# Token-direction sums in plain float32 on four 32-column groups, in place of split fp32r sums that pass through DRAM

## The chip, the cores and the metric

The kernel runs on one core of one Trainium2 chip. The metric is the time on the device in microseconds, from one launch; smaller is better. A measured time is the median over runs; the profile is of one execution.

## The reference

Three stages follow each other: a linear attention, a gated convolution block ("moe"), and a mixing block ("moe2"). The change lies where the second stage ends and the third begins.

```python
# stage 1: B, H, S, D = 4, 8, 576, 64; d_feat = 128
num = einsum('bhsf,bhfd->bhsd', phi(q), einsum('bhsf,bhsd->bhfd', phi(k), v))
x   = (num / den) laid out as [4, 576, 512]
# stage 2: d_ff = 1024
h = maximum(x @ w_in, 0);  c = 3-tap convolution of h along the tokens
x = (h * sigmoid(c)) @ w_out                      # [4, 576, 512]
# stage 3: rank R = 32, hidden 2048
u = x + ((x^T @ U) @ V)^T                         # U [576, 32], V [32, 576]
out = u + maximum(u @ w_ch1, 0) @ w_ch2
```

`x^T @ U` sums over all 576 tokens of a batch: for each batch it is a [32, 512] table, here called the token sums T = U^T x. It must be complete before the first row of u of that batch can be made.

## The kernel before

**Number formats.** Most matmuls run in fp32r, a one-pass format that keeps fewer bits; to keep float32 accuracy each operand is split into a high and a low part, and three products (high·high, high·low, low·high) are summed. A matmul on plain float32 operands is also used, in the attention stage; the trace shows it as two matmul instructions for each call in the program.

**Tiles.** The 4 x 576 = 2304 tokens are 18 tiles of 128 rows, 9 for a pair of batches: four tiles of the even batch, one middle tile whose first 64 rows belong to the even batch and last 64 to the odd one, and four tiles of the odd batch.

**Stage 2** is a loop over n = 0..31 (4 batches of 8 blocks of 128 hidden features). In round n `moe_in(n)` makes a block of h, and two rounds later `out_and_sums(n)` calls `moe_out(n)`, which adds the block into four PSUM tiles `x2p`. After the eighth block of a batch `x2_rows` copies each finished tile with ACT to an SBUF tile `x2` and sends it to DRAM (`x2d`). The middle tile of a pair is made by `moe_out_middle` in PSUM tile `x2m`, from the held pieces `ghold`, after the odd batch.

**The token sums before.** `split_t` takes one waiting x2 tile per round, makes its high part `x2h` on ACT and its low part `x2l` on DVE. `flush_t`, in the next round, multiplies: U's tile with its high and low halves side by side (64 columns) against `x2h`, then U's high half (32 columns) against `x2l`, into one PSUM tile `tp`, whose 64 rows DVE copies or adds into the accumulator `tacc` ([64, 512]; two of them, one for even and one for odd batches). For the middle tile this happens twice, once for each batch. When a batch is complete, `tacc` is stored to DRAM (`td`) by a DMA on SP's queue; `load_tstack` loads it back with its two halves side by side into a staging tile `ta`, adds the halves (`tf`), and writes the fp32r stack `tst` (high, low, high) that `mix` multiplies with V.

**Around the seam.** After the loop, stage 3 runs in 5 blocks of 4, 4, 4, 4 and 2 tiles. `mix(i, t)` computes the mixed rows in PSUM tile `ups` and DVE adds them to `u`; `turn(i, t)` transposes `u` on PE into `utp`, and ACT and DVE split it into `uh` and `ul`; `up` and `down` are the two large products (`hps`, and `po`). `between(i, s)` is called between them and places `mix`, `turn`, the last sums and `load_tstack(2)`, `load_tstack(3)`. `tp` shares the two PSUM buffers of `ps_u` with `ups` and `utp` here; in stage 2 it shares the one buffer of `ps_t` with `x2m`.

**Order.** PE's order is that of the program text from the attention stage through the first pass over the blocks (`tc.manual_schedule`). The orders on DVE, ACT and SP's DMA queue are chosen by the framework's planner from its own estimate of times, and each of them is then run strictly in that order. Weights for stage 3 are decoded by `ch_piece`, eight pieces early, in stage 2, and the rest later (`decode`); each piece takes one buffer of the staging tags `raw` and `x` (two buffers each), the same that `load_tstack` uses for `ta` and `tf`.

Of the kernel before, what the change touches and what calls it, by code (L numbers as in the profile page):

```python
# [8 lines left out]
F32 = mybir.dt.float32  # L9
F32R = mybir.dt.float32r  # L10
# [8 lines left out]
P = 128  # L19
# [5 lines left out]
def kernel(  # L25
# [15 lines left out]
    nc = tc.nc  # L41

    B, H, S, D = 4, 8, 576, 64
    DM = H * D
    FF = w_in.shape[1]
    HID = w_ch1.shape[1]
    R = U.shape[1]
    NK = DM // P
    NJ = FF // P
# [8 lines left out]
    cpool = ctx.enter_context(tc.tile_pool(name="cpool", bufs=1))  # L58
    dpool = ctx.enter_context(tc.tile_pool(name="dpool", bufs=1, space=DRAM))
    wpool = ctx.enter_context(tc.tile_pool(name="wpool", bufs=8, side="right"))  # L60
    stage = ctx.enter_context(tc.tile_pool(name="stage", bufs=2))
# [3 lines left out]
    make_identity(nc, ident)  # L65

    cw = cpool.tile([P, 3 * NJ], F32, name="cw")
    us = [cpool.tile([P, 5, 2 * R], F32R, name=f"us{i}") for i in range(2)]

    td = [dpool.tile([2 * R, DM], F32, name=f"td{b}") for b in range(B)]  # L70
    x2d = [dpool.tile([P, DM], F32, name=f"x2d{i}") for i in range(NT)]
    NU = B * H // 4
    PT = 2 * S
# [71 lines left out]
    def load_us(odd):  # L145
        if odd:
            parts = [
                (everything, slice(R, 5 * R), U[LEFT:S].rearrange("(t p) r -> p t r", p=P)),
                (slice(LEFT, P), slice(0, R), U[0:LEFT]),
            ]  # L150
            zero = (slice(0, R),)
        else:
            parts = [
                (everything, slice(0, 4 * R), U[0:MAIN].rearrange("(t p) r -> p t r", p=P)),
                (slice(0, LEFT), slice(4 * R, 5 * R), U[MAIN:S]),
            ]
            zero = (slice(4 * R, 5 * R),)
        f = load_small(P, 5 * R, f"us{odd}", parts, zero).rearrange("p (t r) -> p t r", r=R)
        nc.vector.tensor_copy(us[odd][:, :, 0:R], f)
        nc.vector.tensor_sub(us[odd][:, :, R : 2 * R], f, us[odd].bitcast(F32)[:, :, 0:R])  # L160

    def split_steps(src, hi, lo, name, engine):

# [101 lines left out]
    raw, state, xt = {}, {}, {}  # L265
# [298 lines left out]
    i = NU - 1  # L564
# [20 lines left out]

    vpool = ctx.enter_context(tc.tile_pool(name="vpool", bufs=1, side="right"))
    vst = vpool.tile([3 * R, S + P], F32R, name="vst")
    taccs = [vpool.tile([2 * R, DM], F32, name=f"tacc{i}") for i in range(2)]
    moe_ctx = ExitStack()
    mpool = moe_ctx.enter_context(tc.tile_pool(name="mpool", bufs=1, side="right"))  # L590
    ps_x = moe_ctx.enter_context(tc.tile_pool(name="ps_x", bufs=4, space=PSUM))
    ps_t = moe_ctx.enter_context(tc.tile_pool(name="ps_t", bufs=1, space=PSUM))
# [43 lines left out]
    def x2_rows(b, gt, ps):  # L636
        if b == B - 1 and gt % 9 > 4:
            x2 = x2_last[:, gt % 9 - 5, :]
        else:
            x2 = mpool.tile([P, DM], F32, tag="x2", name=f"x2_{gt}", bufs=5)  # L640
        nc.scalar.copy(x2, ps)
        nc.sync.dma_start(out=x2d[gt], in_=x2)
        t_todo.append((b, gt, x2))

    def moe_out(n):
        b, j = divmod(n, NJ)
        if j == 0:
            x2p[:] = [ps_x.tile([P, 512], F32, tag="x", name=f"x2p{b}_{t}") for t in range(4)]
        g = gs.pop(n)
        off = LEFT * (b % 2)  # L650
        rest = MAIN - off * (MAIN // LEFT)
        nc.gpsimd.tensor_copy(  # L652
            ghold[:, :, j, off : off + LEFT], g.bitcast(F32)[:, :, rest : rest + LEFT]
        )
        w = [wout[j // 2][:, x, (j % 2) * 512 : (j % 2) * 512 + 512] for x in range(2)]
        for t in range(4):
            ts_ = slice(off + t * P, off + (t + 1) * P)
            for i, (gi, wi) in enumerate(((0, 0), (0, 1), (1, 0))):
                nc.tensor.matmul(  # L659
                    x2p[t], lhsT=g[:, gi, ts_], rhs=w[wi],  # L660
                    start=(j == 0 and i == 0), stop=(j == NJ - 1 and i == 2),
                )
        if j == NJ - 1:
            for t in range(4):
                x2_rows(b, (b // 2) * 9 + (b % 2) * 5 + t, x2p[t])

    middle = {}

    def moe_out_middle(pair, js):
        if pair not in middle:  # L670
            middle[pair] = ps_t.tile([P, 512], F32, tag="t", name=f"x2m{pair}")
        ps = middle[pair]
        for j in js:
            for gi, wi in ((0, 0), (0, 1), (1, 0)):
                nc.tensor.matmul(  # L675
                    ps, lhsT=ghold[:, gi, j, :], rhs=wout[j // 2][:, wi, (j % 2) * 512 : (j % 2) * 512 + 512],
                    start=(j == 0 and gi + wi == 0), stop=(j == NJ - 1 and gi == 1),
                )
        if js[-1] == NJ - 1:
            x2_rows(2 * pair + 1, 9 * pair + 4, ps)  # L680

    t_todo = []

    t_split = []

    def split_t(pool, bufs):
        if t_todo:

            t_todo.sort(key=lambda e: e[1])
            b, gt, x2 = t_todo.pop(0)  # L690
            xh = pool.tile([P, DM], F32R, tag="x2h", name=f"x2h_{gt}", bufs=bufs)
            xl = pool.tile([P, DM], F32R, tag="x2l", name=f"x2l_{gt}", bufs=bufs)
            nc.scalar.copy(xh, x2)
            nc.vector.tensor_sub(xl, x2, xh.bitcast(F32))
            t_split.append((b, gt, xh, xl))

    def flush_t(psum, tag):
        if t_split:
            b, gt, xh, xl = t_split.pop(0)
            r = gt % 9  # L700
            if r < 4:
                parts = [(b, us[0][:, r, :], r == 0)]
            elif r == 4:
                parts = [(b - 1, us[0][:, 4, :], False), (b, us[1][:, 0, :], True)]
            else:
                parts = [(b, us[1][:, r - 4, :], False)]
            for bb, ut, first in parts:
                tacc = taccs[bb % 2]
                pt = psum.tile([P, 512], F32, tag=tag, name=f"tp{gt}_{bb}")
                nc.tensor.matmul(pt[0 : 2 * R], lhsT=ut, rhs=xh, start=True, stop=True)  # L710
                nc.tensor.matmul(pt[0:R], lhsT=ut[:, 0:R], rhs=xl, start=False, stop=True, skip_group_check=True)
                if first:
                    nc.vector.tensor_copy(tacc, pt[0 : 2 * R])
                else:
                    nc.vector.tensor_add(tacc, tacc, pt[0 : 2 * R])
                if (r == 4 and bb == b - 1) or r == 8:
                    nc.sync.dma_start(out=td[bb], in_=tacc)

    def load_vst():
        for c in range(2):  # L720
# [8 lines left out]
    tstack = []  # L729

    def load_tstack(b):
        ta = stage.tile([P, 2, DM], F32, tag="raw", name=f"ta{b}")[0:R]
        nc.sync.dma_start(out=ta, in_=td[b].rearrange("(a r) d -> r a d", a=2))
        tf = stage.tile([P, DM], F32, tag="x", name=f"tf{b}")[0:R]
        nc.vector.tensor_add(tf, ta[:, 0, :], ta[:, 1, :])
        st = vpool.tile([3 * R, DM], F32R, tag="tst", name=f"tst{b}", bufs=2)
        nc.vector.tensor_copy(st[0:R], tf)
        nc.vector.tensor_copy(st[2 * R : 3 * R], tf)
        nc.vector.tensor_sub(st[R : 2 * R], tf, st.bitcast(F32)[0:R])
        tstack.append(st)  # L740

    LAG = 2

    def out_and_sums(n):
        moe_out(n)
        if n == 2 * NJ - 1:
            moe_out_middle(0, range(NJ))
        if n < B * NJ - 1:
            flush_t(ps_t, "t")
            split_t(mpool, 2)  # L750

    early = {n: divmod(i, 2) for i, n in enumerate((9, 12, 14, 17, 20, 22, 24, 27))}
    for n in range(B * NJ):
        b, j = divmod(n, NJ)
# [29 lines left out]
    left = ctx.enter_context(tc.tile_pool(name="left", bufs=1))  # L784
    ps_u = ctx.enter_context(tc.tile_pool(name="ps_u", bufs=2, space=PSUM, side="right"))
# [45 lines left out]
    def prep(i, s):  # L831

        if 0 < s <= sizes[i]:
            turn(i, s - 1)
        if s < sizes[i]:
            mix(i, s)
# [4 lines left out]
    last, pair = B * NJ - 1, B // 2 - 1  # L841
# [64 lines left out]
    pend = None  # L906
    todo = [(j, c) for j in coming[0] for c in range(2)]

    splits, flushes = ((0, 0), (0, 5), (0, 7), (1, 5), (1, 6)), ((0, 1), (0, 6), (1, 0), (1, 6), (1, 7))

    def between(i, s):
        if (i, s) in flushes:
            flush_t(ps_u, "u")
        if (i, s) in splits:
            split_t(left, 1)
        if i + 1 < NB:
            prep(i + 1, s - 1) if s else None
        if (i, s) in ((0, 3), (1, 7)):
            load_tstack(2 + i)

    with tc.manual_schedule(engines={mybir.EngineType.PE}):
        begin(2, wpool)
# [75 lines left out]
```

## Time and profile before

| what | us |
|---|---|
| median of 3 runs | 813.12 (812.91 to 817.39) |
| span of the profiled execution | 813.1 |
| PE busy with matmuls | 797.3 (98%) |
| DVE busy | 534.4 (66%) |
| ACT busy | 360.9 (44%) |
| mean granted TensorE clock | 0.995 |

The span reaches from the first to the last instruction; the profiled execution stands within 0.1 us of the median. A PE matmul's length in the rows is its latency; matmuls overlap, so the distance between two starts is what one costs. An idle time in brackets at a row's end is what the engine waited before it, and for whom.

### The profile page before, as it was taken

The numbers are of one execution on the slowest core, as the hardware profiler recorded it, in microseconds if no ns is written. First come the engines' busy times: TensorE is split into PE (matmuls) and PEld (weight loads), VectorE is DVE, ScalarE is ACT, GpSimd is POOL, SyncE is SP. The second block draws the span as 40 slices with busy tenths as digits, with TensorE's granted clock in tenths as the row PEclk, the third lists the DMA queues.
The fourth block names the chain that finished last, engine by engine and source line by source line (L and its number), as shares of the span: only waits on it lengthen the run. The fifth ranks groups of instructions, "written<-read, shape, count | busy, mean of one in ns | idle before, by whom it ended". The sixth has DMA issues, their size and how long they took to land.

```text
span 813.1 us, 12709 instructions
## 1 busy us (share of the span) xinstructions
PE 797.3 (98%) x5086; PEld 644.6 (79%) x5086; DVE 534.4 (66%) x849; ACT 360.9 (44%) x643; POOL 120.4 (15%) x112
## 2 busy tenths in 40 slices
PE   8999999999999999999899999999999999999997
PEld 5666666669998888988678778888888888888886
DVE  5777877856999986884445795884387276231322
ACT  4778877766687564553322332441142132101010
POOL 0344445530216521110000000000000000000000
PEclk8999999999999999999999999999999999999999
DMA  7355555412212110202700231230021020000212
GB/s 228 108 166 162 160 155 170 132 32 82 67 66 92 30 69 14 69 23 71 233 8 1 65 96 34 79 104 0 29 76 52 1 78 27 0 1 1 87 69 78
DMA packets 36442, 61.27 MB, mean 75 GB/s; under 512 B 7264, under 2 KB 21728, under 8 KB 36384
## 3 DMA queue, kind: packets, MB, share of 16 engines
q1 hardware_dynamic: 36096, 60.37, 23.6%
q8 instruction: 40, 0.66, 0.3%
q14 instruction: 18, 0.15, 0.1%
q10 hardware_dynamic: 288, 0.09, 0.0%
HBM read 50.34 MB, written 10.04 MB: 74 GB/s over the span
## 4 chain that ended last, share of the span: by engine, by line
PE 58%; DVE 9%; DMA 4%; ACT 1%; issue 1%; DVEq 0%; ACTq 0%; SPq 0%
PE po L888 22%; PE hps L866 22%; PE x2p L659 6%; PE hp L611 6%; DVE cv L623 1%; PE x2m L675 1%; DMA c_5r<-in_moe_w_ch_dram 1%; DVE g L631 1%; PE utp L825 1%; DMA td<-tacc 1%; DVE u L893 1%; DMA c_0r<-in_moe_w_ch_dram 1%; DVE cv L628 1%; DMA c_4r<-in_moe_w_ch_dram 0%; DMA c_3r<-in_moe_w_ch_dram 0%
## 5 line engine op out<-in xcount | busy, mean ns | idle before, releaser
L872 ACT ACTIVATE hh<-hps 128x512 fp32r<-128x512 f32 (+1 forms) x80 | 44.2, 552 | 211.8 <-PE hps L866 207.0
L873 DVE SCALAR_TENSOR_TENSOR hl<-hps,hh 128x512 fp32r<-128x512 f32 (+1 forms) x80 | 50.6, 632 | 95.7 <-ACT hh L872 95.7
L611 PE MATMUL hp<-xh,win 128*128 128x288 f32 x512 | 105.6, 295 | 0.0
L659 PE MATMUL x2p<-wout,g 128*128 128x512 f32 x384 | 96.2, 392 | 1.6 <-ACT g L630 1.6
L866 PE MATMUL hps<-uh,c1h 128*128 128x512 f32 (+1 forms) x240 | 88.9, 370 | 1.1 <-ACT uh L828 1.1
L866 PE MATMUL hps<-ul,c1h 128*128 128x512 f32 (+1 forms) x240 | 88.5, 369 | 0.1
L866 PE MATMUL hps<-uh,c1l 128*128 128x512 f32 (+1 forms) x240 | 88.4, 368 | 0.0
L611 PEld LDWEIGHTS hp<-xh,win 128*128 128x128 f32 x512 | 84.2, 188 | 3.8 <-issue 0.5
L888 PE MATMUL po<-c2h,hh 128*128 128x512 f32 x216 | 84.3, 390 | 0.0
L888 PE MATMUL po<-c2l,hh 128*128 128x512 f32 x216 | 84.3, 390 | 0.0
L893 DVE TENSOR_TENSOR u<-u,po 128x512 f32<-128x512 f32 x90 | 58.5, 679 | 38.2 <-PE po L888 38.2
L888 PE MATMUL po<-c2h,hl 128*128 128x512 f32 x216 | 82.0, 389 | 0.0
L659 PEld LDWEIGHTS x2p<-wout,g 128*128 128x128 f32 x384 | 69.7, 188 | 14.4 <-ACT g L630 1.8
L611 PE MATMUL hp<-xl,win 128*128 128x288 f32 x256 | 75.6, 295 | 0.0
L652 POOL CAST ghold<-g 128x128 fp32r<-128x128 f32 x32 | 43.1, 1355 | 147.0 <-DVE g L631 140.9
L623 DVE SCALAR_TENSOR_TENSOR cv<-h,cw,cv 128x576 f32<-128x576 f32 x64 | 51.5, 810 | 8.9 <-ACT cv L621 8.5
L866 PEld LDWEIGHTS hps<-uh,c1h 128*128 128x128 f32 x240 | 45.2, 188 | 9.0 <-ACT uh L828 1.3
L866 PEld LDWEIGHTS hps<-ul,c1h 128*128 128x128 f32 x240 | 45.2, 188 | 8.3 <-DVE ul L829 0.5
L866 PEld LDWEIGHTS hps<-uh,c1l 128*128 128x128 f32 x240 | 45.3, 189 | 7.9
L611 PEld LDWEIGHTS hp<-xl,win 128*128 128x128 f32 x256 | 48.2, 188 | 1.2
L888 PEld LDWEIGHTS po<-c2h,hl 128*128 128x128 f32 x216 | 40.6, 188 | 8.6
L888 PEld LDWEIGHTS po<-c2l,hh 128*128 128x128 f32 x216 | 40.6, 188 | 8.0
(490 smaller groups left out, 1486.9 us busy)
## 6 DMA issues: line engine op xcount, KB each, us to landing
v<-in_v_dram SPq DMA_DIRECT2D x8, 640.0 KB, 5.7
kr<-in_k_dram SPq DMA_DIRECT2D x24, 192.0 KB, 3.7
qr<-in_q_dram SPq DMA_DIRECT2D x24, 192.0 KB, 3.8
rb<-recd SPq DMA_DIRECT2D x32, 144.0 KB, 3.7
u<-x2d SPq DMA_DIRECT2D x18, 256.0 KB, 4.2
out_dram<-u SPq DMA_DIRECT2D x18, 256.0 KB, 2.1
x2d<-x SPq DMA_DIRECT2D x14, 256.0 KB, 2.0
c_0r<-in_moe_w_ch_dram SPq DMA_DIRECT2D x2, 512.0 KB, 4.0
```

Of the source, the lines that this page charges most:

```text
L611: nc.tensor.matmul(ps[:, 0:HC], lhsT=win[kk][:, wi, j * P : (j + 1) * P], rhs=xs[b][kk][xi][:, cs], start=(i == 0), stop=(i == 3 * NK - 1),)
L623: nc.vector.scalar_tensor_tensor(out=cv, in0=h[:, t : t + S], scalar=cw[:, t * NJ + j : t * NJ + j + 1], in1=cv, op0=ALU.mult, op1=ALU.add,)
L628: nc.vector.tensor_mul(cv, cv, h[:, 1 : S + 1])
L631: nc.vector.tensor_sub(g[:, 1, :], cv, g.bitcast(F32)[:, 0, :])
L652: nc.gpsimd.tensor_copy(ghold[:, :, j, off : off + LEFT], g.bitcast(F32)[:, :, rest : rest + LEFT])
L659: nc.tensor.matmul(x2p[t], lhsT=g[:, gi, ts_], rhs=w[wi], start=(j == 0 and i == 0), stop=(j == NJ - 1 and i == 2),)
L675: nc.tensor.matmul(ps, lhsT=ghold[:, gi, j, :], rhs=wout[j // 2][:, wi, (j % 2) * 512 : (j % 2) * 512 + 512], start=(j == 0 and gi + wi == ...
L866: nc.tensor.matmul(ps[:, 0:w], lhsT=ch[j, 0][wi][:, kc], rhs=x[:, kk, :], start=(n == 0), stop=(n == 3 * NK - 1))
L872: nc.scalar.activation(hh, ps[:, 0:w], AF.Relu)
L873: nc.vector.scalar_tensor_tensor(out=hl, in0=ps[:, 0:w], scalar=0.0, in1=hh.bitcast(F32), op0=ALU.max, op1=ALU.subtract)
L888: nc.tensor.matmul(po[i][t], lhsT=x[:, cs], rhs=w, start=(j == js[0] and n == 0), stop=(j == js[-1] and n == 2))
L893: nc.vector.tensor_add(u, u, p)
```

## The change

It replaces `split_t` and `flush_t` by one helper, `token_sums`. U is kept as one plain float32 tile `us` with ten 32-column pieces. When the four tiles of a batch are done, four plain float32 matmuls are issued, each with its own 32 columns of U as weights and its own `x2` tile as moving data, and each into its own 32 partitions of one PSUM tile. DVE then copies the first 32 rows to `tacc` and adds the other three. The middle tile is one matmul with 64 columns (both batches' pieces), and two adds. `tacc` is [32, 512], and `load_tstack` reads it directly: no `td`, no `ta`, no `tf`. The calls come one round after their tiles are queued; for the last batch and the last middle tile they stand at `between(0, 1)` and `between(0, 3)`, and `load_tstack(2)` and `load_tstack(3)` both at `between(0, 3)`.

```diff
-    us = [cpool.tile([P, 5, 2 * R], F32R, name=f"us{i}") for i in range(2)]
-    td = [dpool.tile([2 * R, DM], F32, name=f"td{b}") for b in range(B)]
+    us = cpool.tile([P, 10, R], F32, name="us")
...
-        nc.vector.tensor_copy(us[odd][:, :, 0:R], f)
-        nc.vector.tensor_sub(us[odd][:, :, R : 2 * R], f, us[odd].bitcast(F32)[:, :, 0:R])
+        nc.vector.tensor_copy(us[:, 5 * odd : 5 * odd + 5, :], f)
...
-    taccs = [vpool.tile([2 * R, DM], F32, name=f"tacc{i}") for i in range(2)]
+    taccs = [vpool.tile([R, DM], F32, name=f"tacc{i}") for i in range(2)]
...
+            sums_todo.append((b, 0, t_todo[-4:]))          # in moe_out, at j == NJ - 1
...
+            sums_todo.append((2 * pair, 1, t_todo[-1:]))   # in moe_out_middle, at its end
...
-    def split_t(pool, bufs):
...
-    def flush_t(psum, tag):
...
+    def token_sums(psum, tag):
+        if not sums_todo:
+            return
+        b, both, x2s = sums_todo.pop(0)
+        pt = psum.tile([P, 512], F32, tag=tag, name=f"tp{b}_{both}")
+        if both:
+            nc.tensor.matmul(
+                pt[0 : 2 * R], lhsT=us[:, 4:6, :].rearrange("p t r -> p (t r)"), rhs=x2s[0], start=True, stop=True
+            )
+            for i in range(2):
+                nc.vector.tensor_add(taccs[i], taccs[i], pt[i * R : (i + 1) * R])
+        else:
+            for t, x2 in enumerate(x2s):
+                nc.tensor.matmul(
+                    pt[t * R : (t + 1) * R], lhsT=us[:, 6 * (b % 2) + t, :], rhs=x2, start=True, stop=True
+                )
+            tacc = taccs[b % 2]
+            nc.vector.tensor_copy(tacc, pt[0:R])
+            for t in range(1, 4):
+                nc.vector.tensor_add(tacc, tacc, pt[t * R : (t + 1) * R])
...
     def load_tstack(b):
-        ta = stage.tile([P, 2, DM], F32, tag="raw", name=f"ta{b}")[0:R]
-        nc.sync.dma_start(out=ta, in_=td[b].rearrange("(a r) d -> r a d", a=2))
-        tf = stage.tile([P, DM], F32, tag="x", name=f"tf{b}")[0:R]
-        nc.vector.tensor_add(tf, ta[:, 0, :], ta[:, 1, :])
+        tf = taccs[b % 2]
...
     def out_and_sums(n):
+        due = len(sums_todo)
         moe_out(n)
         if n == 2 * NJ - 1:
             moe_out_middle(0, range(NJ))
-        if n < B * NJ - 1:
-            flush_t(ps_t, "t")
-            split_t(mpool, 2)
+        if due:
+            token_sums(ps_t, "t")
...
-    splits, flushes = ((0, 0), (0, 5), (0, 7), (1, 5), (1, 6)), ((0, 1), (0, 6), (1, 0), (1, 6), (1, 7))
...
-        if (i, s) in flushes:
-            flush_t(ps_u, "u")
-        if (i, s) in splits:
-            split_t(left, 1)
+        if (i, s) in ((0, 1), (0, 3)):
+            token_sums(ps_u, "u")
...
-        if (i, s) in ((0, 3), (1, 7)):
-            load_tstack(2 + i)
+        if (i, s) == (0, 3):
+            load_tstack(2)
+            load_tstack(3)
```

## Rows read from the trace of the kernel before

**Rows 1.** The page: span, and the granted clock in 40 slices (tenths).

```profile
span 813.1 us, 12709 instructions
...
PEclk8999999999999999999999999999999999999999
```

**Rows 2.** Two stretches: length; busy PE, PEld, DVE, ACT, POOL (instructions); clock; DMA share, GB/s.

```profile
237.00:277.00 40.00, 38.48 (x232) 34.46 (x231) 39.77 (x66) 29.24 (x55) 24.89 (x6) 1.00 0.25 80
...
452.00:486.00 34.00, 31.54 (x147) 25.29 (x146) 31.74 (x56) 13.40 (x23) 0.00 (x0) 1.00 0.27 82
```

**Rows 3.** Groups of PE's matmuls: shapes, count | busy us, mean ns.

```profile
L711 PE MATMUL tp<-x2l,us 128*32 128x512 f32 x20 | 7.9, 394 | 0.0
L710 PE MATMUL tp<-x2h,us 128*64 128x512 f32 x20 | 7.8, 392 | 0.0
```

**Rows 4.** PE in order of time around one flush: start, length, instruction.

```profile
419.30 0.39 PE L710 MATMUL tp<-x2h,us 128*64 128x512 f32 x1
419.53 0.40 PE L711 MATMUL tp<-x2l,us 128*32 128x512 f32 x1
419.76 0.39 PE L888 MATMUL po<-c2h,hh 128*128 128x512 f32 x1
```

**Rows 5.** PE in order of time: two plain-float32 blocks on four column groups.

```profile
64.52 2.37 PE L355 MATMUL zp<-ek,ones 128*32 128x256 f32 x40
66.81 0.94 PE L291 MATMUL ppk<-w,kr 64*128 64x128 f32 x12
...
75.06 2.15 PE L434 MATMUL dp<-et,z 128*32 128x288 f32 x32
77.14 0.94 PE L291 MATMUL ppq<-w,qr 64*128 64x128 f32 x12
```

**Rows 6.** PE, window 64.45 to 64.75 alone: what started in it.

```profile
64.52 0.42 PE L355 MATMUL zp<-ek,ones 128*32 128x256 f32 x4
```

**Rows 7.** PE after the last such block: three fp32r matmuls.

```profile
181.92 0.53 PE L611 MATMUL hp<-xh,win 128*128 128x288 f32 x2
182.29 0.29 PE L611 MATMUL hp<-xl,win 128*128 128x288 f32 x1
```

**Rows 8.** PE: matmuls that started late, and two ordinary rows behind the first.

```profile
277.06 0.73 PE L659 MATMUL x2p<-wout,g 128*128 128x512 f32 x2 [1.59 <-ACT g L630]
277.63 0.43 PE L611 MATMUL hp<-xh,win 128*128 128x288 f32 x2
277.90 0.29 PE L611 MATMUL hp<-xl,win 128*128 128x288 f32 x1
...
396.91 0.51 PE L866 MATMUL hps<-uh,c1h 128*128 128x512 f32 x1 [1.07 <-ACT uh L828]
...
401.55 0.50 PE L812 MATMUL ups<-tst,vst 96*128 96x512 f32 x1 [0.31 <-DVE tacc L715]
...
412.34 0.66 PE L825 MATMUL utp<-ident,u 128*128 128x128 f32 x4 [0.49 <-DVE u L817]
...
459.03 0.50 PE L813 MATMUL ups<-tst,vst 96*128 96x512 f32 x1 [1.31 <-DVE tst L739]
...
484.94 0.66 PE L825 MATMUL utp<-ident,u 128*128 128x128 f32 x4 [1.04 <-DVE u L817]
```

**Rows 9.** Instructions of tiles x2l and tacc: count, ns min/median/max, first and last start.

```profile
L694 DVE TENSOR_TENSOR x2l<-x,x2h x14: 671/675/791, 243.8 to 396.4; 128x512 fp32r<-128x512 f32 x14
...
L715 DVE TENSOR_TENSOR tacc<-tacc,tp x16: 669/678/681, 257.3 to 448.7; 64x512 f32<-64x512 f32 x16
```

**Rows 10.** ACT in order of time before stage 3's first large product.

```profile
395.75 0.62 ACT L693 CAST x2h<-x 128x512 fp32r<-128x512 f32 x1
396.28 0.58 ACT L828 CAST uh<-utp 128x512 fp32r<-128x512 f32 x1
```

**Rows 11.** SP's DMA queue in order of time, 449 to 455.

```profile
449.37 0.45 SPq L717 DMA_DIRECT2D td<-tacc  x1
...
452.03 2.97 SPq L168 DMA_DIRECT2D c_4r<-in_moe_w_ch_dram  x2
```

More of the change, by code (lines that the diff above doesn't have):

```diff
@@ L642, in x2_rows @@
         nc.sync.dma_start(out=x2d[gt], in_=x2)
-        t_todo.append((b, gt, x2))
+        t_todo.append(x2)
     def moe_out(n):
@@ L680, in moe_out_middle @@
             x2_rows(2 * pair + 1, 9 * pair + 4, ps)
-    t_todo = []
-    t_split = []
-    def split_t(pool, bufs):
[L687 to L695, printed above, removed]
@@ L697, in flush_t @@
-    def flush_t(psum, tag):
[L698 to L717, printed above, removed]
+            sums_todo.append((2 * pair, 1, t_todo[-1:]))
@@ new lines @@
+    t_todo, sums_todo = [], []
+    def token_sums(psum, tag):
[18 more added lines that the diff above has]
+                nc.vector.tensor_add(tacc, tacc, pt[t * R : (t + 1) * R])
```

## The prediction

> **What bounds the kernel now.** I read the page first: the granted clock is at its full step in nearly every slice, so no time is to be won there [rows 1]. PE is busy for 98% of the span, so time falls only where PE gets less to do or waits less. I then read PE's own waits in order of time [rows 8]. From 181.92 us, where stage 2 begins, to the end, PE waits noticeably at seven places; the reader is to see in six of them (the seventh, of 1.3 us at 387 us for the first rows read back from `x2d`, is not touched) that an instruction of the old token sums, or one queued behind them, stands close by. Last I read what DVE, ACT and SP did just before those waits [rows 2, 9, 10, 11].
>
> **PE's work that goes.** The 18 tiles make 20 flushes (each middle tile makes two) of two fp32r matmuls: 40 matmuls [rows 3]. In PE's order each costs 0.23 us: 419.30, 419.53, then the next product at 419.76 [rows 4]. That is 40 x 0.23 = 9.2 us, all on PE's path.
>
> **PE's work that comes.** Four calls with four 32-column matmuls, two with one 64-column matmul. The trace has plain float32 on four column groups: 40 instructions of 256 columns take from 64.52 to 66.81, 2.29 us; 32 of 288 columns take from 75.06 to 77.14, 2.08 us [rows 5]. Four start together at 64.52, and nothing else starts until 64.75 [rows 6], so they go in waves of four: ten waves and eight. With k us a column and a fixed part o, 2560 k + o = 2.29 and 2304 k + o = 2.08: k = 0.00082, o = 0.19. A wave of 512 columns is then 0.42 us (0.46 with o = 0), and a call, two instructions for each matmul, is two waves: 0.84 us. Behind such a block the first fp32r matmuls are late as well: the third starts 0.37 us after the first [rows 7], where two such steps otherwise take 0.27, from 277.63 to 277.90 [rows 8]: 0.10. The entry is not resolved in my rows; I put the same 0.10, between 0 and the whole o. A call costs 0.84 + 0.19 + 0.10 + 0.10 = 1.2 us. A middle call has one group alone, with the same two instructions one behind the other, so it costs the same. Six calls: 7.1 us; PE saves **2.1 us**. The bounds are 6 x 0.84 = 5.0 (saving 4.2), if entering and leaving cost nothing, and the serial case among the rivals.
>
> The fixed part speaks against the change, since six short blocks pay it six times. The Trainium skill says so too (TensorEngine Tiling (Array Packing), Key Properties): changing the tiling mode drains TensorE. The 0.19 and 0.10 us of rows 5 and 7 fit that; by the rule PE's new work is the 7.1 us, without it 5.0.
>
> **What goes on ACT, DVE and SP.** 18 `x2h` copies on ACT (0.6 us each) and 18 `x2l` subtractions on DVE, 0.67 us each [rows 9, 10]; 2 subtractions of U; 4 `tf` adds; 4 stores and 4 loads on SP. The accumulations stay 20 (before 20; after 4 copies, 12 adds, and 4 adds for the middle tiles), of the same width and so the same 0.68 us [rows 9], but come in bursts of four. None of it costs time by itself; it counts where PE waits for it:
>
> - 277.06, 1.59 us: PE waits for g, at the end of a stretch in which DVE is busy 39.77 of 40 us [rows 2, 8]. The four `x2l` of batch 0 lie in it; without them DVE is 2.4 to 2.7 us earlier, while PE comes only 4 x 0.46 - 1.2 = 0.6 us earlier. The wait goes: -1.6.
> - 396.91, 1.07 us for `uh`: on ACT the `x2h` of the middle tile starts 0.53 us ahead of it [rows 8, 10]: -0.5.
> - 401.55, 0.31 us: the middle tile's two `tp` hold both buffers of `ps_u`, so `ups` waits for `tacc` [rows 8]. Now the call takes one: -0.3.
> - 412.34, 0.49 us: `u` stands on DVE behind `tf` and `tst`, which waited for `td` and back. That trip is gone: -0.5.
> - 459.03, 1.31 us: `mix` of the second middle tile waits for `tst` of the last batch, whose sums are stored only at 449.37 [rows 8, 11]. They are now complete some 45 us earlier: -1.3.
> - 484.94, 1.04 us: DVE is busy 31.74 of 34 us before it, with decoding [rows 2, 8]. The `c_4` load is issued only at 452.03, behind the round trip in SP's queue and behind `ta`, which holds a staging buffer [rows 11]. Both are gone, so the planner can decode earlier, where DVE has room: -1.0. If it does not, 0.
>
> An idle time is counted from the end of the last matmul's 0.39 us, of which only 0.23 cost PE time [rows 4]; each of the six waits that vanishes or shortens gives back up to 0.16 us more: -0.9 in all. Sum: -1.6 - 0.5 - 0.3 - 0.5 - 1.3 - 1.0 - 0.9 = -6.1.
>
> **What comes as waits.** At `between(0, 3)` three users (`tp`, `utp`, `ups`) take turns in two buffers, so `ups` waits for both adds: the result about 0.2 us after PE's issue, then 2 x 0.68, less the 0.5 us that PE spends on leaving the block and on four transposes: +1.0. Behind PE stand `mix` and the next `up`. At `between(0, 1)` a copy and three adds (2.7 us) stand on DVE ahead of the add to `u` that the next `turn` wants; `up` covers about 2.7 us of it on PE, so +0.3, and 1 us without that cover. In stage 2 the same bursts have a round of some 6 us. `load_tstack(3)` now waits for its `tst` buffer until `mix(2, 0)`; DVE's order is planned, and its reader comes 30 us later, so 0. Sum +1.3.
>
> **Sum.** 813.1 - 2.1 - 6.1 + 1.3 = 806.2 us. The profiled span equals the median within 0.1 us, so this is also the time that a run would show.
>
> **The rivals.**
> 1. *The waits come back elsewhere.* The orders on DVE, ACT and SP are planned anew: bursts of adds and earlier decoding may put an add to `u` late at the seam, where PE takes every 2.7 us something that DVE must finish. For it: DVE is full in the stretches of rows 2 and the planner's times are estimates. Against: the work removed is larger than what is added. It is decided where a critical DVE step stands behind more than one step of other work (0.68 us each). Time: 813.1 - 2.1 = 811.0 when all gains on waits are lost; 809 to 812. The Trainium skill names this (same page, PSUM Bottleneck): packing the array speeds up TensorE but not the evacuation of PSUM. Before, no run of four evacuations in a row is in the rows, so they cannot tell.
> 2. *All waits go, and the switch is cheap.* 813.1 - 4.2 - 6.1 = 802.8, with the new waits covered by the planner; 802 to 804.9.
> 3. *The four groups do not run side by side (slower).* With four different 512-column tiles as moving data the four could go one after the other: 4 x (8 x 0.42 + 0.39) + 2 x 1.2 = 17.4 us, 8.2 more than before. Against it: rows 6, where the groups also have their own moving data. For it: no row has 512 columns. If the waits still shrink by 4.8 the time is 816.5; if they do not, 821.3. It decides from a call of about 2.3 us on, (9.2 + 4.8)/6.
> 4. *Nothing changes on PE's path*, because the planner fills the freed DVE time with other work and the bursts cost as much as the trips: that is rival 1 at its upper end.
>
> **How the numbers follow.** The forecast's mechanism (804.5 to 808.5) gets 0.5, rival 1 0.25, rival 2 0.2, rival 3 0.05. The predicted time is 806.2. The range goes from rival 2's 802.0 to rival 1's 811.5 and leaves out rival 3 and the outer parts of the others. About 1% (8.1 us) is what a measurement of this kernel can tell from no change: faster than 805.0 are rival 2 and a fifth of the forecast's band, 0.3; slower than 821.2 is half of rival 3 at most, 0.02; the rest is 0.68.
>
> **What would show it.** PE: two waves of four, 0.42 us apart, six blocks, and some 0.3 us lost around each (if the waves are 0.84 apart or single, rival 3). No wait for g near 275 us, none for `tst` near 457, no `ta`. The `c_4` load well ahead of 450 us, and DVE clearly under 31.74 of 34 us in that stretch. One new wait of `ups` for `tacc` of about 1 us at `between(0, 3)`. The forecast is wrong if the wait near 484 stays (then 807.4), or if new waits over 3 us appear in the 20 us after the seam.

## The result and the profile after

| what | before | after |
|---|---|---|
| median, us | 815.12 (812.91 to 817.39, 4 runs) | 807.08 (806.66 to 807.75, 4 runs) |
| ratio | 1 | 0.9908 (95%: 0.9885 to 0.9931) |
| span of the profiled execution, us | 813.1 | 806.0 |
| first `hp` to first `hps` (stage 2), us | 214.99 | 211.53 |
| first `hps` to the end (stage 3), us | 416.15 | 413.83 |

The change gives 0.9% (0.7 to 1.2% by the interval); 806.2 us was forecast. The last two lines are what the change can touch, and they fall by 5.78 us together. The rest of the 7.1 us by which the spans differ lies ahead of the first `hp`, where the start of the program is the same. There PE ran at the half clock for longer in the profile of before. Two windows, the first row of before and the second of after (length; PE, PEld, DVE, ACT, POOL; granted clock; DMA share, GB/s):

```profile
13.40:17.00 3.60, 3.60 (x26) 1.96 (x25) 1.07 (x3) 0.00 (x0) 0.00 (x0) 0.63 0.63 189
```

```profile
13.40:17.00 3.60, 3.60 (x36) 2.43 (x34) 2.27 (x4) 0.58 (x1) 0.00 (x0) 1.00 0.68 217
```

PE makes 36 matmuls there at full clock and 26 otherwise. That belongs to the execution, not to the kernel: run again, before had the shorter stretch and its first `hp` at 180.85, after again at 180.87. All parts below are therefore compared from the first `hp` on.

**The six calls.** By the page after, PE is busy for 793.3 us (797.3 before). PE in order of time around one call of four (start, length, instruction), and around a middle call:

```profile
246.99 0.40 PE L657 MATMUL x2p<-wout,g 128*128 128x512 f32 x1
247.32 1.06 PE L697 MATMUL tp<-x,us 128*32 128x512 f32 x8
248.31 0.40 PE L609 MATMUL hp<-xh,win 128*128 128x288 f32 x1
...
310.51 0.29 PE L609 MATMUL hp<-xl,win 128*128 128x288 f32 x1
310.73 1.07 PE L690 MATMUL tp<-x,us 128*64 128x512 f32 x2
311.74 0.54 PE L609 MATMUL hp<-xh,win 128*128 128x288 f32 x2
```

Eight instructions take as long as two, 1.0 us from the block's first start to the next product's: the four groups do run side by side.

**The waits.** PE's waits of after by releaser (total us, times, longest), those from stage 2 on, then four rows of PE that answer to [rows 8]:

```profile
PE utp L808 <- DVE u L800: 2.8, 2, 1.5
...
PE ups L799 <- DVE tacc L694: 1.0, 1, 1.0
PE hps L849 <- ACT uh L811: 0.7, 1, 0.7
...
PE x2p L657 <- ACT g L628: 0.2, 1, 0.2
```

```profile
269.59 0.42 PE L609 MATMUL hp<-xh,win 128*128 128x288 f32 x2
270.18 0.73 PE L657 MATMUL x2p<-wout,g 128*128 128x512 f32 x2 [0.16 <-ACT g L628]
...
406.02 0.47 PE L799 MATMUL ups<-tst,vst 96*128 96x512 f32 x1 [0.98 <-DVE tacc L694]
...
453.03 0.66 PE L808 MATMUL utp<-ident,u 128*128 128x128 f32 x4 [1.48 <-DVE u L800]
```

Of the wait for g [rows 2, 8] 0.16 us is left, at 270; those near 401, 412, 457 and 484 us are gone. Two are new: 1.0 us for `tacc` at 406, and 1.5 us at 453 for the add to `u` of the second middle tile. (The other of the two `utp` waits, at 383 us, was there before, at 387.) The `x2p` that waits for g is the 157th of 384 in both traces, but in before 420 `hp` matmuls stand ahead of it and in after 392: in stage 2 PE's order differs between the two traces, although it was described above as that of the program text. So a change of order is a rival for this wait; the unread splits below speak to it. The windows show where DVE got its time back [rows 2]:

```profile
237.00:277.00 40.00, 39.84 (x241) 35.24 (x240) 39.91 (x65) 29.77 (x56) 8.71 (x8) 1.00 0.21 72
...
452.00:486.00 34.00, 32.97 (x157) 27.37 (x158) 17.91 (x30) 7.25 (x13) 0.00 (x0) 1.00 0.00 0
```

Ahead of 277 DVE is as full as before, and yet PE hardly stands still: in the same 40 us DVE now makes the low part of g eight times, where before it did so six times, and g comes early enough. Ahead of 486 DVE went from 31.74 to 17.91 us.

**Why PE waits at 453.** The view of the chain that ended last, in order of time around the new wait, a DMA and DVE's pieces behind it:

```profile
443.65 0.61 DVE c L176
444.26 0.02 issue
444.27 3.73 DMA c_6r<-in_moe_w_ch_dram
448.00 0.02 issue
448.02 0.43 DVE c_6x L77
448.45 0.59 DVE u L876
449.05 0.60 DVE hl L856
449.65 0.60 DVE c_6x L80
...
452.38 0.61 DVE u L800
452.99 0.04 issue
453.03 0.66 PE utp L808 x4
```

The step of `c_6` that begins at 448.02 stands in DVE's order ahead of the adds that PE needs. It waits for its DMA, which was issued as soon as the decoding step that began at 443.65 had ended. Everything behind it on DVE stands too, although most of it wants nothing of `c_6`. Between it and the add at 452.38 stand the adds of `po`, an `hl` and two more steps of `c_6`; the three steps of `c_6` take 1.4 us together. The add is late, and PE waits 1.5 us for it.

### The profile page after: what moved, and what is told of

Its sections match the earlier page's. It is cut to its first block, busy times and chain, and to the rows that moved or that the text cites. A ratio compares the mean times of both kernels' runs of the same rounds, so it can differ in the third digit from the quotient of the medians.

```text
span 806.0 us, 12654 instructions
## 1 busy us (share of the span) xinstructions
PE 793.3 (98%) x5082; PEld 640.1 (79%) x5082; DVE 521.5 (65%) x825; ACT 351.8 (44%) x625; POOL 104.5 (13%) x112
## 4 chain that ended last, share of the span: by engine, by line
PE 92%; DVE 3%; DMA 2%; ACT 1%; issue 1%; SPq 0%; DVEq 0%; POOL 0%; ACTq 0%; POOLq 0%
PE hps L849 23%; PE po L871 23%; PE hp L609 13%; PE x2p L657 10%; PE kvp L339 4%; PE np L407 4%; PE ppk L289 3%; PE ppq L289 2%; PE zp L353 2%; PE tq L319 2%; PE dp L432 2%; PE x2m L674 1%; PE utp L808 1%; PE pk L374 1%; DMA c_5r<-in_moe_w_ch_dram 1%
## 5 line engine op out<-in xcount | busy, mean ns | idle before, releaser
L650 POOL CAST ghold<-g 128x128 fp32r<-128x128 f32 x32 | 26.7, 840 | 167.9 <-DVE g L629 160.9
```

The costliest lines, as they stand in the source:

```text
L650: nc.gpsimd.tensor_copy(ghold[:, :, j, off : off + LEFT], g.bitcast(F32)[:, :, rest : rest + LEFT])
```

## The experiments

Two theories. By the first (A), the gain has three sources: PE's shorter work (2.0 us), DVE's relief ahead of the wait for g, and the trip through DRAM that is gone; it was cut by a wait that comes from DVE's new order (453) and by one that the calls bring (406). By the rival (B), the time hangs on the four groups alone, or on the trip alone, and the two new waits are only seen, not paid. In the runs below, the budget is counted as in the table: stage 2, stage 3, and their sum (before 631.14, after 625.36).

**Both kernels again.** Unchanged.

> The kernel before, unchanged, for a second profile. Of the 7.1 us between the two profiled spans, 1.3 lie ahead of the first hp, where the two kernels are the same. Theory (the start-up differs from run to run, by how long the half clock is granted there): stage 1 ends between 179 and 183 us and stages 2 and 3 take 631.1 us within 0.5. Rival (the kernel before itself varies behind the start): stages 2 and 3 differ by 1 us or more from 631.1.

> The changed kernel, unchanged, for a second profile and a time beside the kernel before on one chip. Theory: stages 2 and 3 take 625.4 us within 0.5, whatever the start-up, and the ratio is 0.991 within 0.002. Rival (its waits vary): 1 us or more off.

Before had 215.04 and 416.89, sum 631.93, and 814.89 us in one run: 0.8 us above 631.14, more than the 0.5 expected and less than the rival's 1. After had 211.39 and 413.67, sum 625.06; 807.16 us (806.57 to 809.48, 4 runs), 0.9926 (0.9900 to 0.9951) of the before measured beside it. So a sum repeats within 0.8 us, and smaller differences are not read on their own.

**The old sums without the trip.** Split sums as before; the halves are added on DVE from `tacc`, without `td` and `ta`:

```diff
-                if (r == 4 and bb == b - 1) or r == 8:
-                    nc.sync.dma_start(out=td[bb], in_=tacc)
...
-        ta = stage.tile([P, 2, DM], F32, tag="raw", name=f"ta{b}")[0:R]
-        nc.sync.dma_start(out=ta, in_=td[b].rearrange("(a r) d -> r a d", a=2))
+        tacc = taccs[b % 2]
         tf = stage.tile([P, DM], F32, tag="x", name=f"tf{b}")[0:R]
-        nc.vector.tensor_add(tf, ta[:, 0, :], ta[:, 1, :])
+        nc.vector.tensor_copy(tf, tacc[R : 2 * R])
+        nc.vector.tensor_add(tf, tf, tacc[0:R])
```

> The old split sums with their 40 fp32r matmuls and 18 splits stay; only the way through DRAM goes: the two halves of tacc are added on DVE without td and ta. My theory (the trip cost waits): the waits for tst near 459 (1.6 us between starts) and for u near 412 (0.9) go, those for g near 277 and for uh near 397 stay, so the span falls by 2 to 3.5 us against the kernel before. Rival (the trip was covered, the gain of the change is PE's work and the splits): the span falls by less than 1 us, and the waits come back under other names.

Stage 2 214.79, stage 3 413.56, sum 628.35; 812.02 us (810.85 to 812.34), 0.9963 (0.9948 to 0.9977). The trip alone is worth 2.8 us of the sum, nearly all of it in stage 3. PE's waits (first the view by releaser, then two places in order of time):

```profile
PE utp L822 <- DVE u L814: 2.1, 3, 1.2
PE x2p L658 <- ACT g L629: 1.5, 1, 1.5
...
PE hps L863 <- ACT uh L825: 1.1, 1, 1.1
PE ups L809 <- DVE tacc L714: 0.3, 1, 0.3
```

```profile
400.88 0.40 PE L710 MATMUL tp<-x2l,us 128*32 128x512 f32 x1
401.59 0.50 PE L809 MATMUL ups<-tst,vst 96*128 96x512 f32 x1 [0.31 <-DVE tacc L714]
...
411.60 0.39 PE L863 MATMUL hps<-ul,c1h 128*128 128x512 f32 x1
411.83 0.60 PE L822 MATMUL utp<-ident,u 128*128 128x128 f32 x4
```

The wait near 412 and that for `tst` are gone; those for g, for `uh` and at 401 stay: they do not come from the trip. This run shows two things more. `c_4` is loaded at 330 us (452 in before), and PE's wait near 484 is 0.30 us in place of 1.04, so the trip did hold up that load, as the forecast said, though DVE is still busy for 32.53 us of 452 to 486. And a wait of 0.60 us for `u` has come at 456.79, with decoding steps of `c_4` among the steps ahead of that add on DVE.

**The splits put back, unread.** The kernel after, with 13 of the `x2h` copies (ACT) and `x2l` subtractions (DVE) made again, their results unused; and a second version without the `tensor_sub`, so with the copies alone. In both the work is only added:

```diff
+    def dead_split(pool, bufs):
+        if dead:
+            x2 = dead.pop(0)
...
+            nc.scalar.copy(xh, x2)
+            nc.vector.tensor_sub(xl, x2, xh.bitcast(F32))
...
         if due:
             token_sums(ps_t, "t")
+        if n < B * NJ - 1:
+            dead_split(mpool, 2)
```

> The changed kernel with the splits of 13 x2 tiles of stage 2 put back as work that nobody reads: x2h on ACT and x2l on DVE, one tile a round as before. Theory (the splits made DVE late, and so g): the wait for g before x2p near 270 comes back with 1 to 1.8 us, and stage 2 (first hp to first hps) is 1 to 2 us longer than the 211.5 of the changed kernel. Rival (the wait near 277 went because the planner ordered stage 2 anew): stage 2 within 0.5 us.

> As the run with both halves of the splits put back, but only the copies x2h on ACT, without x2l on DVE. Theory (DVE, busy 39.9 of 40 us there, sets g, not ACT): the wait for g stays under 0.6 us and stage 2 within 0.5 us of the changed kernel's 211.5. Rival (ACT's copies count as much): 1 us or more longer.

With both: stage 2 214.79, stage 3 414.0, sum 628.79, 3.4 above after; 811.05 us (808.93 to 813.97, 10 runs), 0.9952 (0.9933 to 0.9970). With the copies alone: 211.06 and 413.7, the same as after within what repeats, and 808.3 us in one run. So DVE's part of the split costs the time and ACT's none. PE in order of time where the first version loses it, and the same place with the copies alone:

```profile
273.41 0.29 PE L609 MATMUL hp<-xl,win 128*128 128x288 f32 x1
275.63 0.86 PE L658 MATMUL x2p<-wout,g 128*128 128x512 f32 x2 [1.93 <-ACT g L628]
276.30 0.68 PE L609 MATMUL hp<-xh,win 128*128 128x288 f32 x2
276.77 0.44 PE L609 MATMUL hp<-xl,win 128*128 128x288 f32 x1
```

```profile
274.45 0.29 PE L609 MATMUL hp<-xl,win 128*128 128x288 f32 x1
274.58 0.63 PE L658 MATMUL x2p<-wout,g 128*128 128x512 f32 x2
```

The wait for g is back, larger than before (1.93 against 1.59 us [rows 8]): this `x2p` starts 95.1 us after the first `hp`, as in before, and PE, with less work, is there 0.4 us earlier. It is the 157th `x2p`, and 420 `hp` stand ahead of it in both of these runs, as in before. With the copies alone it does not wait, so PE's order is not what takes the wait away. Behind the wait in the first version three matmuls take 0.24 us each instead of 0.13, as the windows show (columns as above):

```profile
240.00:276.00 36.00, 34.07 (x206) 29.85 (x205) 35.91 (x59) 24.67 (x49) 17.16 (x3) 1.00 0.24 76
276.00:279.50 3.50, 3.50 (x16) 3.40 (x15) 3.30 (x8) 3.50 (x9) 1.35 (x4) 0.51 0.00 0
279.50:290.00 10.50, 10.50 (x63) 9.53 (x63) 9.81 (x19) 6.10 (x11) 5.46 (x3) 1.00 0.03 7
```

For 3.4 us the granted clock is the half one: about 13 steps, each 0.107 us longer, 1.4 us. So the wait beyond the ordinary step, 2.1, and the clock, 1.4, make up the 3.4 us within what repeats. The expectation was exceeded in both of its numbers: the wait is 1.93 us (1 to 1.8 expected), and stage 2 is longer by 3.3 (1 to 2 expected); the half clock had not been thought of.

**All on one group of columns.** The four matmuls accumulate in the same 32 partitions of PSUM, so they cannot run side by side; one copy is left of the copy and three adds:

```diff
-                    pt[t * R : (t + 1) * R], lhsT=us[:, 6 * (b % 2) + t, :], rhs=x2, start=True, stop=True
+                    pt[0:R], lhsT=us[:, 6 * (b % 2) + t, :], rhs=x2, start=(t == 0), stop=(t == 3)
...
-            for t in range(1, 4):
-                nc.vector.tensor_add(tacc, tacc, pt[t * R : (t + 1) * R])
```

> The changed kernel with the four matmuls of a call on one and the same 32-column group, summed in PSUM, so that eight instructions go one behind the other; one copy to tacc is left of the copy and three adds. Theory (a wave of four groups costs what one instruction costs, 0.43 us): a call takes 8 x 0.43 + 0.1 + 0.1 + 0.1 = 3.75 us between its neighbours instead of 1.2, four calls cost 10.3 us more on PE, span about 815 to 816 against 806.0, less up to 1 us for DVE's fewer adds. Rival (the groups share a limit, and side by side saves little): under 5 us more.

Stage 2 218.63, stage 3 416.27, sum 634.90, 9.5 above after; 817.26 us (815.99 to 818.72, 10 runs), 1.0025 (1.0010 to 1.0041). PE in order of time at one call:

```profile
247.25 3.62 PE L697 MATMUL tp<-x,us 128*32 128x512 f32 x8
250.80 0.40 PE L609 MATMUL hp<-xh,win 128*128 128x288 f32 x1
```

Eight starts 0.43 us apart, 3.55 us for the call where after needs 1.00. Four calls cost 4 x 2.55 = 10.2 us more; the small waits for g that after still has, 0.6 us in all, are gone in this run, which leaves about the 9.5 measured. Plain float32 without the side-by-side placing would have lost to before.

**The two new waits, taken away one by one and together.** First, the middle call and `load_tstack` are moved from `between(0, 3)` to `between(0, 6)`:

```diff
-        if (i, s) in ((0, 1), (0, 3)):
+        if (i, s) in ((0, 1), (0, 6)):
             token_sums(ps_u, "u")
-        if (i, s) == (0, 3):
+        if (i, s) == (0, 6):
             load_tstack(2)
             load_tstack(3)
```

Second, DVE's steps on `c_6` are ordered behind the last `mix` of the block, so that nothing that `mix` needs stands behind their DMA or behind the steps themselves:

```diff
-        nc.vector.tensor_add(u, u, ps)
+        mixed[gt] = nc.vector.tensor_add(u, u, ps)
...
-                    ch_piece(6, n - 1)
+                    with tc.issue_after(mixed[15].ins):
+                        ch_piece(6, n - 1)
```

Third, both. Fourth, both, and the last two calls next to each other (the edit against the third):

```diff
-        if (i, s) in ((0, 1), (0, 6)):
+        if (i, s) == (0, 6):
+            token_sums(ps_u, "u")
             token_sums(ps_u, "u")
```

> The changed kernel with the last middle sum and the two load_tstack moved from between(0, 3) to between(0, 6), where no mix and no turn wants a buffer of ps_u. Theory (three users take turns in two buffers): the 1.2 us between utp and ups near 405 go and nothing takes their place, span about 804.8 against 806.0. Rival (DVE is late there in any case): a wait of over 0.8 us stays or comes back within 40 us, span 805.6 or more.

> The changed kernel with the DVE steps of the two pieces of c_6 queued behind the last mix of block 3. Theory (the wait of 1.6 us for u near 453 is head-of-line blocking: on DVE the first step of c_6 stands ahead of the adds to u and waits for a DMA that lands late): that wait goes, span about 804.4 against 806.0. Rival (the four adds of the finished block alone make it late): a wait of 1 us or more stays at that place, span 805.5 or more.

> Both moves together, middle sum at between(0, 6) and c_6 behind block 3's last mix. Theory: the two waits are independent and their gains add, span about 803.2 against 806.0. Rival (PE being earlier makes DVE late elsewhere): less than 1.5 us.

> The version with both moves (middle sum at between(0, 6), c_6 behind block 3's last mix), with the call for the last batch moved there too, so that the two calls stand side by side on PE. Theory (each block pays a fixed part on entering and leaving): one such part, 0.3 to 0.4 us, and the 0.17 us that ups waits near 400 go, stage 3 about 410.6 against 411.05. Rival (six evacuations in a row on DVE make PE wait): stage 3 longer by 0.5 us or more.

| kernel | stage 2 | stage 3 | sum | median, us (range) | ratio (95%) |
|---|---|---|---|---|---|
| after | 211.53 | 413.83 | 625.36 | 807.08 (806.66 to 807.75) | 0.9908 (0.9885 to 0.9931) |
| first | 211.03 | 412.39 | 623.42 | 807.02 (805.81 to 808.42) | 0.9904 (0.9886 to 0.9923) |
| second | 211.75 | 412.17 | 623.92 | 806.56 (804.84 to 807.43) | 0.9893 (0.9875 to 0.9911) |
| both | 211.5 | 411.05 | 622.55 | 805.13 (803.88 to 805.34) | 0.9877 (0.9863 to 0.9892) |
| fourth | 211.36 | 410.69 | 622.05 | 804.83 (803.40 to 805.94) | 0.9866 (0.9837 to 0.9895) |

In stage 3 the two edits give 1.44 and 1.66, and 2.78 together: they add up, and together they equal the two waits as counted between starts (1.19 + 1.64 = 2.83). Of the medians, those of the last two stand clear of after by their ranges, while the intervals of their ratios still touch that of after; the single edits are seen in the stage rather than in the median. The spans expected were 804.8, 804.4 and 803.2 for the first three, and 804.0, 805.2 and 803.4 were measured; of the 0.8 us by which the second is over, 0.6 lie ahead of its first `hp`. The second edit takes away the stand for the DMA and the three steps of `c_6` ahead of the add together, and no run separates these two. PE in order of time with both edits, at the places of the two waits:

```profile
403.29 0.39 PE L873 MATMUL po<-c2h,hl 128*128 128x512 f32 x1
403.52 0.60 PE L810 MATMUL utp<-ident,u 128*128 128x128 f32 x4
403.88 0.48 PE L799 MATMUL ups<-tst,vst 96*128 96x512 f32 x1
...
450.27 0.39 PE L851 MATMUL hps<-ul,c1h 128*128 128x512 f32 x1
450.50 0.60 PE L810 MATMUL utp<-ident,u 128*128 128x128 f32 x4
450.86 0.47 PE L795 MATMUL ups<-tst,vst 96*128 96x512 f32 x1
```

No brackets, and the ordinary 0.23 us ahead of each `utp`. The fourth kernel has the lowest median of all and 0.36 us less in stage 3 than the third, which is no more than what repeats; the two cannot be told apart. Its two calls follow each other without a product between them:

```profile
412.60 1.07 PE L697 MATMUL tp<-x_last,us 128*32 128x512 f32 x8
413.59 1.07 PE L690 MATMUL tp<-x,us 128*64 128x512 f32 x2
414.60 0.50 PE L873 MATMUL po<-c2h,hh 128*128 128x512 f32 x1
```

The first still takes 0.99 us up to the second's start, though both are plain float32: going from 32-column to 64-column pieces does not spare the way out of the block. What is spared is the late fp32r product behind the first call and the entry of the second, 0.2 us in all.

Theory A holds in the parts that were tested: the trip (2.8 us), the split on DVE (3.4), the side-by-side groups (9.5 if absent) and the two waits (2.8) each have their own price. B falls: neither the groups nor the trip explains the time alone. PE's own 2.0 us are counted in the traces, and no run takes them away by themselves. The prices are not parts of one sum that gives the 5.78 us: the 3.4 hold 1.4 of half clock, which neither before nor after pays there, and where PE waits for g its shorter work ahead of that place only makes the wait longer.

## Why the prediction was right

The forecast's mechanism came true; one term of its sum failed, and the start of the program, which the change does not touch, made up for most of it.

- **PE's work: 2.1 forecast, 2.0 measured.** The second wave starts 0.453 us after the block's start, and the next product 0.43 + 0.09 us behind that wave's last start. The block is entered 0.10 late (247.32 where 247.22 would be the ordinary step behind 246.99), is 0.996 us long, and the first products behind it lose 0.10: 1.2 us, the forecast's number. Six times that is 7.19, and before it was 9.22. (The forecast's terms add up to 1.23 a call, so to 7.4 and a saving of 1.8; it wrote 7.1 and 2.1, and the slip took it nearer to the measurement.) The bound of 5.0 would have been wrong, and so would the serial case: one group costs 3.55 us a call. The Trainium skill has for column packing (TensorE: Matmul & The Clock Gate, Measured speedup vs the span model; 32 columns of weights, 512 of moving data) 2.38 times for three tiles; no run here has three, and with four the trace shows 3.55 against 1.00 us, entry into the block not counted.
- **The wait for g: -1.6 and up to 0.16 more forecast, -1.25 measured.** Counted between starts it was 1.86 and is now 0.43 + 0.18 at two earlier places. The cause is as named: the unread splits on DVE bring it back, the copies on ACT do not.
- **The waits of the trip: near 412 and near 457, -1.8 forecast, -2.45 measured** between starts (0.89 and 1.56), with 0.9 in the forecast's own term for counting. The kernel without the trip shows them gone for this reason.
- **`uh` and 401: -0.8 forecast, -1.0 measured** (1.78 to 1.26, and 0.48 to 0). They stay in the kernel without the trip, so it is not the trip that made them; that it is the split and the second `tp`, as the forecast had it, is likely by what is left, but no run put these back alone.
- **The wait near 484: -1.0 forecast, -1.2 measured.** DVE is far from full there, as the forecast said, and the kernel without the trip loads `c_4` early too and keeps 0.30 of the 1.04 us. A wait of 0.3 us at 466 went as well, which the forecast had not listed.
- **The new wait at `between(0, 3)`: +1.0 forecast, +1.19 measured**, at the place and for the tile named; at `between(0, 1)` 0.17 for 0.3. The row at 406.02 shows a PSUM buffer that is held until two adds of 0.68 us each have read it. The rule that the forecast weighed says that packing speeds up TensorE but not the evacuation of PSUM (the Trainium skill, TensorEngine Tiling (Array Packing), PSUM Bottleneck); the call at 406.02 is not a packed one, and behind the packed call at `between(0, 1)`, with a copy and three adds, PE lost only the 0.17 us.
- **What comes as waits: +1.3 forecast, +3.0 measured; this is the step that failed.** The two waits that it named were right. The third, 1.64 us at 453, comes with the same earlier decoding that took away the wait near 484: steps of `c_6`, the first of them behind its own DMA, stand in front of the add that the last `mix` needs. The forecast had asked whether the planner could decode earlier; it had not asked what stands in DVE's strict order behind a decoding step whose weights have not landed. (It is rival 1 in kind, a DVE step that stands behind other work at the seam, at a fraction of that rival's price, and behind a DMA rather than a burst of adds.) SP's queue in order of time shows how late the weights come: `c_4` moved from 452 [rows 11] to 327 us, but `c_5` and `c_6` followed only at 431 and 444.

```profile
326.90 3.69 SPq L166 DMA_DIRECT2D c_4r<-in_moe_w_ch_dram  x2
...
431.42 0.94 SPq L166 DMA_DIRECT2D c_5r<-in_moe_w_ch_dram  x2
444.27 2.26 SPq L166 DMA_DIRECT2D c_6r<-in_moe_w_ch_dram  x2
```

- **The sum.** From stage 2 on the forecast had -2.1 - 6.1 + 1.3 = -6.9; the trace has -5.78. All waits together, between starts, fell by 3.15 where 4.8 were forecast, and the difference of 1.65 is the wait at 453. PE's 2.03 and these 3.15 leave 0.6 us of the 5.78 that stands in no wait and no call; it stays unplaced, and the sums of equal kernels differ by as much.
- **The base.** In spans, 806.2 + 1.65 (the wait) - 0.6 (unplaced) - 1.3 (the half clock at the start) gives the 806.0 of the trace: the close hit has that 1.3 us in it, which is no work of the change but luck. And the forecast took the profiled span for the time of a run. In fact a run's time stands about 2 us above its span, 807.75 for the 806.0 of after and 814.89 for the 812.8 of the repeated before, so the span of 813.1 does not belong to a run of 813.12 us, as the forecast and the table ahead of it had it.

## What to carry to other kernels

A helper computation that is small on PE may still be dear by what it puts on the engines beside it: the larger gains here were DVE work that stood ahead of a product, and a trip through DRAM that others queued behind. Packing the small matmuls on column groups paid here even with about 0.3 us lost around each block, as the groups ran side by side and the blocks were few; on one group the kernel was slower than before. When work goes from an engine with a strict order, look at what moves into the freed time, above all at steps that wait for a DMA, and put them behind the steps that the critical engine wants.

## What the hardware showed unexpectedly

- Behind a wait of PE of 1.93 us, with 36 us at full clock ahead of it in which PE was busy for 34.07, the granted clock fell to the half (0.51) for 3.4 us and cost about 1.4 us. Behind the wait of 1.59 us in before [rows 8] it did not fall: 1.00 from 278.00 to 281.50. What decides between the two is not settled here. So that wait cost 1.7 times its own length.
- The half clock at the start of the program differs between executions: 6.83 us in the profile of before, 3.41 in that of after and in both of the repeated kernels. In the two profiles of before the first `hp` stands at 181.92 and 180.85, over 1 us apart, more than some of the edits above bring. The clock rows do not account for all of the start: in the fourth kernel's profile they show no half clock there, and yet its first `hp` stands at 181.32, later than in after.
- The way into and out of a plain-float32 block on column groups costs about 0.3 us (0.10 in, 0.09 at the end, 0.10 on the next products), with one group as with four; between a block of 32-column pieces and one of 64-column pieces the 0.09 is paid as well.
